# Early loading of two transposed h columns, and modulation blocks at groups 0, 1, 3, 4 of the backward middle stage

## The chip, the cores and the metric

The kernel runs on one core of a Trainium2 chip. The metric is the device time of one execution in microseconds (us). All results below are medians of fast runs, and each ratio is the mean time of one kernel's fast runs over the mean of the other kernel's fast runs of the same rounds, on the same chip; so it is not quite the ratio of the medians that stand beside it. The interval in brackets is a 95% interval. A run counts as slow when it is over 1.5% above the fastest of its kernel.

Terms: TensorE does the matrix products, into tiles of PSUM that ScalarE or VectorE then empties; SyncE issues nearly all DMAs (transfers between DRAM and the on-chip memory) here, one after the other. The granted clock is the share of TensorE's full clock in the profile. A filler is a product that is put between others only to keep TensorE busy.

## The reference

The reference runs a block with a Fourier filter and a squared-ReLU network forward, and returns its output and the gradients of nine inputs. Cut to what matters here:

```python
def _A_ref(x, w_r, w_i):                      # Fourier filter over (2048, 512)
    X = rfft2(x.astype(jnp.float32)) * (w_r + 1j * w_i)
    return irfft2(X, s=(S, D)).astype(jnp.bfloat16)

def _B_ref(x, w1, b1, w2, b2):                # D = 512, F = 1792
    h = jnp.einsum('bsd,df->bsf', x, w1) + b1
    r = jnp.where(h > 0, h, 0)
    return jnp.einsum('bsf,fd->bsd', r * r, w2) + b2

mod = (_silu(c) @ w_mod)                      # w_mod is (512, 6*512); six rows sa, ca, ga, sb, cb, gb
h = _layernorm(x) * (1 + ca) + sa;  x = x + ga * _A_ref(h, A_w_r, A_w_i)
h = _layernorm(x) * (1 + cb) + sb;  x = x + gb * _B_ref(h, ...)
# ... and jax.vjp of all this, for grad_out
```

Four parts of the backward pass matter. The **middle stage** runs the Fourier filter backwards in 8 groups of frequencies. Each group produces a gradient gW of the filter, which is stored. Products of the w1 gradient (grad_w1) are put between the groups to keep TensorE busy. The **modulation blocks** compute parts of the gradients of c and of w_mod, one block of 512 columns of w_mod each. **g1** is the inverse transform that follows the middle stage. The **last stage** takes pairs of row tiles, computes the gradient of x, and uses products of the w2 gradient (grad_w2) as TensorE's filler. Those products need transposed columns of h (hn), which a transposing DMA brings from DRAM.

## The kernel before

A modulation block, its two w_mod buffers (wmc) and its two output buffers (gwm):

```python
class GMod:                                   # self.bufs = 2
    def emit(self, jc, q, row, pool, ppool):
        nc.tensor.matmul(psb, lhsT=K["ones_sq"][q:q + 1, :], rhs=row, ...)
        nc.scalar.copy(out=gmbc, in_=psb)                                        # L459
        for dc in range(0, 4, 2):
            wmc = pool.tile([P, 2, D], BF16, name="wmc", bufs=self.bufs)
            nc.sync.dma_start(wmc, self.wm_view[:, dc:dc + 2, cs])               # L463
            gwm = pool.tile([P, 2, D], BF16, name="gwm", bufs=self.bufs)
            for i in range(2):
                if i == 0:
                    nc.scalar.activation(gwm[:, i, :], gmbc, AF.Copy, scale=...) # L467
                else:
                    nc.vector.tensor_scalar(gwm[:, i, :], gmbc, ...)             # L469
                nc.vector.scalar_tensor_tensor(out=junk, in0=wmc[:, i, :], ...,
                                               in1=gmbc, accum_out=...)          # L470 gm_junk
            nc.sync.dma_start(self.out9_view[:, dc:dc + 2, cs], gwm)             # L472
```

psb, the tile of the block's own product (L457), comes from the PSUM pool mmps with its two tiles named mm, which the products of grad_w1 and grad_w2 use, too.

The middle stage. All its loads and stores go through SyncE's one queue. In the profile gW is the gradient of the filter, gw at L1108 that of w1, and gw at L1176 that of w2:

```python
def grad_w1(fb, dc):
    for t in range(NT): nc.tensor.matmul(ps[:, 0:W4], ...)                       # L1104
    nc.scalar.copy(out=w1o[0][:, fb % 2, :], in_=ps[:, 0:W4])                    # L1108, gw1 has 2 buffers
    if fb % 2 == 1: nc.sync.dma_start(out4_view[...], w1o[0]...)                 # L1110
# ...
def ew_b(gi, G):
    cmul(nc, ew, Z[gi], G, ...)               # VectorE, L418 to L421
    gW = ew.tile([P, 2, 2, FP], BF16, name="gW", bufs=3)
    cmul(nc, ew, Xt[gi], G, gW[...], ...)
    for ...: nc.sync.dma_start(rows_, gW[...])                                   # L1146
def after_b(gi):
    if gi + 4 < 8: load(gi + 4)               # Z (L1133) and Xb (L1135)
    if gi == 4: nc.sync.dma_start(K["LG"], LG_dram)
    fill_w1(2 if 0 < gi < 6 else 1)
    if gi % 2 == 1: gms.pop(0)()              # a modulation block at groups 1, 3, 5, 7
```

The seam and the last stage:

```python
nc.sync.dma_start(g_sb, g_view)               # 2 MB, L1196
load_hn()                                     # transposing DMA, 512 KB, L1168
load_rows3(0); load_rows3(2)                  # rows n1 and gxl, L1193, L1194
for _ in range(3): load_hn()
spec_g1(tc, K, Z, CS)                         # L346; VectorE (L351) and ScalarE empty its PSUM tiles
# ... per pair of row tiles: q1 = gh1 * n1 (L1254), grad_w2 (L1173) as filler,
#     load_rows3(t + 4), and after the pair t == 10: grad_b2(), whose closing sum
#     (L1083) needs a ScalarE cast and a VectorE subtraction first
```

## Time and profile before

| | before |
|---|---|
| median of 3 runs | 433.97 us (431.92 to 434.96) |
| profiled span, mean granted TensorE clock | 432.7 us, 0.99 |
| TensorE, VectorE, ScalarE busy | 92%, 82%, 59% |
| last product of g1 ends | 350.36 us |
| last product of TensorE begins | 429.08 us |

A wait line reads: engine, instruction and line that waited, what released it, then total us, count and longest. In a timeline the columns are start, duration, engine, line, operation, output<-input, and in square brackets the idle time ahead with its releaser; SPq is SyncE issuing DMAs. In a table of stretches there follow, after the window, its length, the busy us of TensorE, its weight loads, VectorE, ScalarE and GpSimd (instruction counts in parentheses), the granted clock, the DMA share and GB/s. Two stretches of the kernel before that the prediction doesn't show, and that matter later:

```profile
315.00:325.00 10.00, 9.50 (x60) 5.33 (x58) 6.82 (x18) 2.58 (x6) 0.00 (x0) 1.00 0.96 313
345.00:355.00 10.00, 9.41 (x72) 6.47 (x72) 7.18 (x16) 6.17 (x12) 0.00 (x0) 1.00 0.82 275
```

TensorE is nearly full in both, at full clock.

### The profile page before, as it was taken

The page shows a single profiled execution, that of the slowest core. Times are in us where ns is not written, and L with a number is a line of the kernel's source. Part 1 is how long each engine was busy: PE and PEld are TensorE (multiplying, and loading weights), DVE is VectorE, ACT ScalarE, POOL GpSimd, SP SyncE. Part 2 cuts the span into 40 slices and gives each one's busy share as a digit, 9 for nine tenths or more (in the row PEclk, how much of TensorE's full clock was granted, in tenths as well). Part 3 has the DMA queues.
Part 4 walks back from the last instruction along what each step waited for, and adds up shares of the span by engine and source line. Part 5 has one row for each costly group of instructions (what it writes and reads, how often), then busy time and mean ns, then how long its engine had stood idle before and what let it go on. Part 6 is the DMA issues. An engine that isn't in the chain of part 4 may idle for free.

```text
span 432.7 us, 7098 instructions
## 1 busy us (share of the span) xinstructions
PE 398.7 (92%) x2353; PEld 196.1 (45%) x2375; DVE 353.7 (82%) x864; ACT 256.1 (59%) x487; POOL 40.9 (9%) x114
## 2 busy tenths in 40 slices
PE   2789999999899999999999999999999799995996
PEld 0344446654344444443444344455555464441332
DVE  6889768959995588969897998929577967989796
ACT  5578699679881286348536765465438374545231
POOL 7447930000000000000000000000000000000000
PEclk9999999999999999999999999999999999998899
DMA  9998899969595379779965997997995599999994
GB/s 237 222 293 278 223 282 273 318 222 188 177 360 191 121 127 329 186 162 226 276 189 158 210 330 271 245 244 217 263 300 160 166 245 257 255 257 255 247 246 137
DMA packets 147147, 101.11 MB, mean 234 GB/s; under 512 B 98945, under 2 KB 131590, under 8 KB 146726
## 3 DMA queue, kind: packets, MB, share of 16 engines
q1 hardware_dynamic: 145458, 98.01, 84.6%
q0 software_dynamic: 1088, 2.11, 2.1%
q10 hardware_dynamic: 564, 0.53, 0.4%
q8 instruction: 19, 0.31, 0.3%
q14 instruction: 18, 0.15, 0.1%
HBM read 35.44 MB, written 41.60 MB: 178 GB/s over the span
## 4 chain that ended last, share of the span: by engine, by line
PE 35%; DVE 25%; ACT 14%; DMA 12%; SPq 5%; issue 5%; POOL 2%; ACTq 0%; DVEq 0%
PE og L901 10%; PE mm L872 8%; PE mm L707 5%; PE mm L1173 4%; DMA out_dram<-gW 2%; PE psG L346 2%; ACT gab L712 2%; DVE gm_junk L470 2%; SPq L1168 2%; DMA n<-n_dram 2%; DMA out_dram<-gw 1%; DVE jk L1258 1%; ACT AE L329 1%; DMA y<-gx_dram 1%; DMA out_dram<-x 1%
## 5 line engine op out<-in xcount | busy, mean ns | idle before, releaser
L707 PE MATMUL mm<-gT,w2T 128*128 128x512 bf16 x224 | 57.8, 383 | 3.0 <-ACT gab L712 3.0
L1173 PE MATMUL mm<-g_sb,hn 128*128 128x512 bf16 x217 | 52.8, 394 | 3.3 <-DVE gw L1176 2.9
L872 PE MATMUL mm<-h2T,w 128*128 128x512 bf16 x224 | 53.4, 378 | 1.6 <-ACT r L874 1.4
L1104 PE MATMUL mm<-gab,h_sb 128*128 128x448 bf16 x256 | 51.4, 352 | 0.8 <-ACT gw L1108 0.8
L901 PE MATMUL og<-w1T,gab 128*128 128x512 bf16 x218 | 49.9, 379 | 1.0 <-DVE o L966 0.8
L901 PE MATMUL og<-w,h 128*128 128x512 bf16 x217 | 49.1, 379 | 0.3
L874 ACT ACTIVATE r<-mm,b1col 128x512 bf16<-128x512 f32 x56 | 37.0, 685 | 6.1 <-PE mm L872 3.3
L1173 PEld LDWEIGHTS <-hn 128*128 128x128 bf16 x224 | 21.6, 100 | 30.5 <-issue 8.2
L1104 PEld LDWEIGHTS <-h_sb 128*128 128x128 bf16 x256 | 24.6, 98 | 22.3 <-issue 1.7
L872 PEld LDWEIGHTS <-w 128*128 128x128 bf16 x224 | 21.1, 97 | 30.0 <-issue 8.3
L901 PEld LDWEIGHTS <-h 128*128 128x128 bf16 x224 | 21.8, 98 | 26.1 <-issue 0.9
L901 PEld LDWEIGHTS <-gab 128*128 128x128 bf16 x224 | 21.6, 98 | 25.9 <-issue 1.4
L707 PEld LDWEIGHTS <-w2T 128*128 128x128 bf16 x224 | 21.2, 98 | 22.4 <-issue 6.4
L914 ACT CAST G<-og 128x512 bf16<-128x512 f32 x16 | 9.2, 580 | 28.1 <-PE og L901 28.1
L876 DVE TENSOR_TENSOR h<-r 128x1024 bf16<-128x1024 bf16 x28 | 19.2, 687 | 4.8 <-ACT r L874 4.8
L1253 ACT ACTIVATE gs<-gn,inv 128x512 bf16<-128x512 bf16 x16 | 11.4, 716 | 18.6 <-DVE gn L1251 18.6
L712 ACT CAST gab<-mm 128x512 bf16<-128x512 f32 x36 | 21.4, 600 | 1.7 <-PE mm L707 1.5
L1108 ACT CAST gw<-mm 128x448 bf16<-128x448 f32 x16 | 8.7, 544 | 22.1 <-DMA out_dram<-gw 12.6
L418 DVE TENSOR_TENSOR p<-Z,G 128x1028 bf16<-128x1028 bf16 x8 | 5.6, 697 | 18.7 <-ACT G L313 10.1
L710 DVE CAST gab<-mm 128x512 bf16<-128x512 f32 x20 | 13.8, 688 | 7.3 <-PE mm L707 7.1
L377 ACT ACTIVATE Tsb<-psT 128x512 bf16<-128x512 f32 x32 | 18.5, 604 | 1.8 <-PE psT L375 1.5
L880 DVE TENSOR_TENSOR gab<-r,gab 128x1024 bf16<-128x1024 bf16 x28 | 19.2, 684 | 0.0
(289 smaller groups left out, 779.7 us busy)
## 6 DMA issues: line engine op xcount, KB each, us to landing
h_dram<-h SPq DMA_DIRECT2D x28, 256.0 KB, 3.6
gh_dram<-gab SPq DMA_DIRECT2D x28, 256.0 KB, 4.3
w<-in_B_w_dram SPq DMA_DIRECT2D x2, 1792.0 KB, 8.8
wmc<-in_w_mod_dram SPq DMA_DIRECT2D x12, 256.0 KB, 4.7
out_dram<-gwm SPq DMA_DIRECT2D x12, 256.0 KB, 3.3
wz_dram<-Z SPq DMA_DIRECT2D x8, 258.0 KB, 3.1
xs_dram<-Xs SPq DMA_DIRECT2D x8, 258.0 KB, 3.0
Z<-wz_dram SPq DMA_DIRECT2D x8, 258.0 KB, 4.1
```

The source lines that it names most:

```text
L377: nc.scalar.activation(Tsb, ps, AF.Copy, scale=EF_S)
L707: nc.tensor.matmul(ps, lhsT=w2T[:, dc, fc * P:(fc + 1) * P], rhs=gT[b][:, :, dc, :], start=(dc == 0), stop=(dc == 3))
L710: nc.vector.tensor_copy(out=gaT[b][:, fc, :], in_=ps)
L712: nc.scalar.copy(out=gaT[b][:, fc, :], in_=ps)
L872: nc.tensor.matmul(ps, lhsT=w1[:, dc, (fc + i) * P:(fc + i + 1) * P], rhs=h2T[b][:, :, dc, :], start=(dc == 0), stop=(dc == 3))
L874: nc.scalar.activation(r[:, i, :], ps, AF.Relu, bias=b1col[:, fc + i:fc + i + 1])
L876: nc.vector.tensor_tensor(h2, r, r, op=ALU.mult)
L880: K["gh"] = nc.vector.tensor_tensor(gh, r, gh, op=ALU.mult).ins
L901: nc.tensor.matmul(ps, lhsT=lhs(fc), rhs=rhs[:, fc, :], start=(fc == 0), stop=(fc == NFC - 1))
L1104: nc.tensor.matmul(ps[:, 0:W4], lhsT=h2_sb[:, t, dc * P:(dc + 1) * P], rhs=ghn[t // 4][:, t % 4, fs], start=(t == 0), stop=(t == NT - 1))
L1173: nc.tensor.matmul(ps, lhsT=hns[fc][:, t, :], rhs=g_sb[:, t, :], start=(t == 0), stop=(t == NT - 1))
L1253: nc.scalar.activation(gs[:, i, :], gn[:, i, :], AF.Copy, scale=inv1[:, t + i:t + i + 1], accum_out=rr[:, i, 0:1])
```

## The change

The intent: bring two of the 14 transposed columns while the DMA engines have room (behind the stores of group 5), so that the row loads of the last stage no longer stand behind a transpose at the seam; and move the modulation blocks out of groups 5 and 7, whose tail holds up VectorE and so g1.

```diff
+    hnp = tc.alloc_tile_pool(name="hnp", bufs=1, side="right")
+    hns, endp = [], {}
+    def load_hn():                                    # moved up; first two columns in hnp
+        ...
                 for p0_, n, rows_ in w_parts(o, gi):
-                    nc.sync.dma_start(rows_, gW[p0_:p0_ + n, i, :, 0:DF])
+                    K["gW"] = nc.sync.dma_start(rows_, gW[p0_:p0_ + n, i, :, 0:DF]).ins
 ...
             fill_w1(2 if 0 < gi < 6 else 1)
-            if gi % 2 == 1:
+            if gi == 5:
+                with tc.issue_after(K["gW"]):
+                    load_hn()
+                    load_hn()
+            if gi in (0, 1, 3, 4):
                 gms.pop(0)()
 ...
     nc.sync.dma_start(g_sb, g_view)
-    load_hn()
     load_rows3(0)
     load_rows3(2)
-    for _ in range(3):
+    for _ in range(2):
         load_hn()
```

The pools are cut here.

More of the change, by code (lines that the diff above doesn't have):

```diff
@@ L1049 @@
     gm = GMod(tc, K, scf, gsc, wm_view, out9_view)
+    hnp = tc.alloc_tile_pool(name="hnp", bufs=1, side="right")
+    hns, endp = [], {}
+    def load_hn():
+        fc = len(hns)
+        if fc < NFC:
+            pool = hnp if fc < 2 else endp.get("hn", endp["gw"])
+            hns.append(pool.tile([P, NT, P], BF16, name="hn", bufs=2 if pool is not endp.get("hn") else 4))
+            nc.sync.dma_start(hns[fc], h_dram[fc, :, :], transpose=True)
     lf2 = tc.alloc_tile_pool(name="lf2", bufs=1, side="right")
@@ L1160 @@
     g_sb = gwp.tile([P, NT, D], BF16, name="g_sb")
-    hns, endp = [], {}
-    def load_hn():
-        fc = len(hns)
-        if fc < NFC:
-            hns.append(endp.get("hn", gwp).tile([P, NT, P], BF16, name="hn", bufs=4))
-            nc.sync.dma_start(hns[fc], h_dram[fc, :, :], transpose=True)
+    endp["gw"] = gwp
     def grad_w2(fc):
@@ L1307 @@
     gwp.release()
+    hnp.release()
     h2p.release()
```

## The prediction

> **What bounds the kernel now.** I read the engine totals first: TensorE is busy for 92% of the span, VectorE for 82%. So TensorE's gaps are what a change can win, and the next question is where they lie. I cut the second half into stretches. The columns are busy microseconds of TensorE, its weight loads, VectorE, ScalarE and GpSimd, then the granted clock, the DMA share and GB/s:
>
> ```profile
> 285.00:295.00 10.00, 10.00 (x112) 5.72 (x111) 3.87 (x9) 5.46 (x11) 0.00 (x0) 1.00 0.83 258
> 305.00:315.00 10.00, 10.00 (x70) 5.94 (x68) 5.12 (x12) 5.74 (x11) 0.00 (x0) 1.00 0.96 288
> 325.00:335.00 10.00, 9.66 (x63) 5.64 (x63) 7.47 (x19) 8.83 (x17) 0.00 (x0) 1.00 0.50 144
> 335.00:345.00 10.00, 8.04 (x80) 4.88 (x79) 10.00 (x25) 4.01 (x7) 0.00 (x0) 1.00 0.57 166
> 390.00:398.00 8.00, 3.55 (x24) 1.42 (x23) 7.08 (x17) 4.74 (x11) 0.00 (x0) 0.94 1.13 257
> 398.00:405.00 7.00, 7.00 (x19) 2.18 (x18) 4.65 (x14) 1.83 (x4) 0.00 (x0) 0.58 1.00 268
> ```
>
> The middle stage on the way back runs from about 283 us to 338 us. TensorE is full there, because the products of the w1 gradient fill the gaps between the groups: nothing done inside the stage can shorten it. Its tail (335 to 345) has VectorE full and TensorE not; the DMA engines are half idle from 325 to 345, then full. Around 395 there is a hole in TensorE's work, followed by a lowered clock.
>
> Second, the waits, with the total, the count and the longest:
>
> ```profile
> PE psG L346 <- DVE utcs L351: 1.9, 1, 1.9
> ACT gw L1108 <- DMA out_dram<-gw: 12.6, 2, 7.1
> DVE q L1254 <- DMA gxl<-gx_dram: 2.3, 1, 2.3
> DVE q L1254 <- DMA n<-n_dram: 2.1, 2, 1.1
> PE mm L1173 <- DVE gw L1176: 2.9, 1, 2.9
> ```
>
> The first says that TensorE stands at the inverse transform (g1) because VectorE has not emptied its PSUM tile. The third and fourth say that VectorE, which paces the last stage, waits for rows. The last is the hole at 395.
>
> Third, the chain that ended last, at the seam of the two stages:
>
> ```profile
> 342.25 0.67 DVE gm_junk L470 x2
> ...
> 344.12 0.67 DVE gm_junk L470 x2
> 344.79 0.62 DVE utcs L351
> 345.44 0.60 PE psG L346 x4
> ...
> 348.28 7.24 SPq L1168
> 355.57 1.28 SPq L1193
> 356.90 3.30 DMA gxl<-gx_dram
> 360.20 0.68 DVE q L1254
> ```
>
> This is the heart of it. The fourth modulation block (gm_junk) stands on VectorE ahead of the first emptying of g1, which frees TensorE. Then SyncE needs 7.24 us to issue the first transposed h column (L1168), and the row loads of the last stage (L1193, L1194) are queued behind it; VectorE gets its rows at 360.20.
>
> **What the Trainium skill says.** "Perfetto Trace Analysis", section 'What "DMA-bound" means', counts an issuing engine whose sequencer is solid with DMA slices as a bound of its own. The trace agrees for the last stage: from 358.3 to 417.9 us the 13 remaining column transposes hold SyncE for 8.60+3.76+2.49+5.51+3.93+4.13+4.10+2.48+3.54+2.12 = 40.7 us of 59.6. "DMA: Bandwidth & Descriptors", section "Rules for kernel authors", advises to issue a DMA early and wait for it late, which is this change; section "Issuing engines are not separate DMA queues" says that all DMAs share the same 16 engines, so an early load is free only where these have room (0.50 and 0.57 above, but 0.96 from 305 to 315). "TensorE: Matmul & The Clock Gate", section "What's actually happening", gives the half clock after an idle window of about 3.4 us. The trace fits: gaps of 1.5 and 2.9 us between 391.7 and 398, then a clock of 0.58, and 16 matmuls in 1.86+4.54 = 6.4 us that take 3.6 elsewhere.
>
> **The change part by part.**
> (a) Two of 14 transposes move from the seam to behind the stores of group 5. Each brings 512 KB (128 x 2048 bf16); the record of L1168 has 2.0 to 7.2 us of SyncE, median 3.3, and a median 6.1 us to landing. Group 5's stores end at 333.6 us. Two transposes at 2.5 to 3.3 us (the DMA engines are half free) hold SyncE until about 339.5. Behind them wait the stores of groups 6 and 7 (about 2.5 us of issue each, before: 338.2 to 344.4). SyncE also loses the last modulation block's issues there (about 3 us between 333.7 and 337.4, 1.1 at 344.5). So the stores of group 7 end near 344.5, as before, and the 2 MB load of g_sb, which waited for such a store to land (1.8 us), is issued at 347 to 348, as before (347.87).
> (b) After g_sb the row loads follow at once, so at about 348.5 instead of 355.57: 7 us earlier in issue. They queue in the DMA rings behind g_sb: 2 MB at the 377 GB/s of the stretch 350 to 355 is 5.6 us, so the first rows land at about 355.5. VectorE's q starts there instead of at 360.20, some 4.5 us earlier, if g1 is done in time, which is (c).
> (c) The modulation blocks move from groups 1, 3, 5, 7 to 0, 1, 3, 4. One costs VectorE four products of 0.746, four read-outs of 0.082 and two scalings of 0.348: 4.0 us by the sum, 3.34 us elapsed, since they overlap (331.27 to 334.61). ScalarE pays 0.59+2x0.72 = 2.0 us, TensorE 0.39, and 1 MB is moved. Groups 5 to 7 lose two blocks: VectorE's group 6 can start when its G is there (about 331.5 to 333 instead of 334.61), group 7 ends at about 339.5 instead of 342.2, and the first emptying of g1 starts there instead of at 344.70: 4 to 5 us earlier. TensorE then loses the stalls of 1.95 and 0.45 us in g1, and the transform (now done at 352) is done by about 348, so that the unfolding is no longer what holds q. In groups 0 to 4 the blocks fall where VectorE waits for ScalarE (4.9 us at 306 to 311, 5.25 us at 322 to 327), so they should be hidden.
> (d) The last stage has 12 transposes instead of 14, about 2x3.3 us of SyncE and 1 MB less, while its DMA share is 1.0 to 1.1. So its row loads come earlier, too, and the VectorE waits of 2.1 us on n should shrink.
>
> **The sum.** Only TensorE's gaps can be won. From 337 us to its last product they are 0.45+1.95 (g1), 0.15, 0.44, 1.5, 2.9, plus 6.4-3.6 = 2.8 us lost to the clock: 10.2 us. The floor is 434-10 = 424. The first two, 2.4 us, I count fully. Of the 7.2 us around 391 to 405 (two gaps and the clock) I count half, 3.6: VectorE comes some 4.5 us earlier into the last stage, TensorE some 2.4, so VectorE gains a lead of only 2 us, and it is full from 366 to 397. I take off 0.5 for friction in groups 0 to 4. That is 5.5 us: **428.5 us**.
>
> **Rivals.**
> 1. *SyncE and ScalarE choke in groups 0 to 4.* A block needs two buffers of w_mod columns that the block before must free, and each landing takes 4.7 us. Blocks in adjacent groups (0 and 1, 3 and 4) put such waits into the one queue that also stores gW and the w1 gradient, and ScalarE already waited 7.1 us for one of these stores. The DMA engines stand at 0.96 from 305 to 325. For it: TensorE lost 0.83 us behind that wait. Against it: TensorE always had filler. It would cost 1 to 4 us: 430 to 433.
> 2. *The new transposes hold up SyncE.* If each takes 4 us or more, the stores of group 7 and with them g_sb come 3 to 4 us later, and the rows land where they did. The gain is then the g1 part and a little more: 431.
> 3. *The last stage is bound by TensorE's work or by the DMA engines anyway.* From 405 us on TensorE is full. If the hole at 395 only moves, the earlier start is worth 2.4 to 3 us: 431.
> 4. *The hole closes entirely*, with its clock loss, as VectorE's lead suffices: 424 to 425.
>
> **Range and chances.** Most weight lies between rivals 2 and 3 (431) and rival 4 (424.5), about 428.5 in the middle; rival 1 sets the upper end. Range 424 to 433. Faster by over 2% means below 425.5, nearly the whole of the floor: 0.15. Slower by over 2% would need new stalls of 9 us: 0.03. Within 2%: 0.82.
>
> **What would show it.** Right: no wait of psG on utcs; VectorE's first q at 355 to 357; L1193 issued within 2 us of g_sb; the two early transposes at 333 to 340; about 5 us shorter gaps of TensorE after 337, and its clock nearer to 1 at 395 to 405. Wrong: SyncE's stores of group 7 ending after 346, TensorE below 9.5 in a stretch from 285 to 335, or the wait on gw (2.9 us) still there with the clock loss.

## More of the kernel before

The medians of the kernel before differed between rounds from 432.4 to 434.6 us, which is why ratios and not differences of medians decide.

The diff moves lines: grad_w1 is L1114 after, its ScalarE copy L1118, its store L1120, the gW stores L1156, the transposes L1058, the rows L1201 and L1202, g_sb L1204, grad_w2 L1181, its scaling by VectorE L1184, the closing sum of b2 L1093, q L1261. The block keeps its lines (L457 to L472), and so does g1 (L346, L351).

## The result and the profile after

The change made the kernel slower: 440.13 us (439.95 to 441.8, 4 runs) against 434.46 us (431.92 to 434.96, 4 runs), ratio 1.0151 [1.0103, 1.0199]. The predicted 428.5 us, and its range up to 433, were missed on the slow side. The same work is done (TensorE 399.6 us busy, before 398.7); the time is in new gaps. From the start of the middle stage (283 us) to the end of g1, TensorE's gaps of 0.4 us or more add up to 9.0 us, before 3.2 us. g1 ends at 357.03 us instead of 350.36, 6.7 us later, and the last product begins at 434.40 instead of 429.08, 5.3 us later: the last stage gives 1.4 us back. The order of instructions on each engine is not the same in the two kernels: with the blocks other things moved. After the end of g1 48 products of the w1 gradient are left instead of 37, and in the last stage some products of grad_w2 and of the b2 sum stand at other places.

The stretches of the kernel after:

```profile
315.00:325.00 10.00, 5.75 (x23) 2.63 (x23) 4.03 (x12) 4.93 (x9) 0.00 (x0) 0.83 0.94 247
335.00:345.00 10.00, 10.00 (x77) 6.37 (x75) 7.79 (x20) 5.42 (x11) 0.00 (x0) 1.00 0.49 150
345.00:355.00 10.00, 5.33 (x48) 3.56 (x46) 8.12 (x17) 2.12 (x5) 0.00 (x0) 0.83 0.86 177
```

TensorE stands for over 4 us in two of them, and each time the clock falls as well. The prediction's own sign of failure, "TensorE below 9.5 in a stretch from 285 to 335", is there in the first. The waits of the kernel after in the second half name both gaps and what led to them:

```profile
DVE gm_junk L470 <- DMA wmc<-in_w_mod_dram: 9.0, 3, 3.6
ACT gw L1118 <- DMA out_dram<-gw: 8.6, 2, 6.6
ACT gwm L467 <- DMA out_dram<-gwm: 4.9, 3, 3.3
PE psG L346 <- DVE utcs L351: 4.7, 1, 4.7
PE mm L1114 <- ACT gw L1118: 4.3, 1, 4.3
DVE gwm L469 <- DMA out_dram<-gwm: 3.6, 2, 2.6
```

The first, third and sixth line hardly exist in the kernel before (none of them reaches 0.5 us there). All three are waits of a modulation block for its buffers: VectorE for w_mod columns to land, ScalarE and VectorE for the gwm store of the block before. The fourth was 1.9 us and the fifth 0.8 us before. The second is not new: before, ScalarE waited 12.6 us for these stores.

**The first gap, read backwards.** Two lines of ScalarE's timeline and four of SyncE's, kernel after:

```profile
302.76 0.72 ACT L467 ACTIVATE gwm<-gmbc,scf 128x512 bf16<-128x512 bf16 x1 [3.26 <-DMA out_dram<-gwm]
...
318.67 0.53 ACT L1118 CAST gw<-mm 128x448 bf16<-128x448 f32 x1 [6.58 <-DMA out_dram<-gw]
```

```profile
294.51 4.32 SPq L1156 DMA_DIRECT2D out_dram<-gW  x6
...
299.40 0.91 SPq L472 DMA_DIRECT2D out_dram<-gwm  x2
...
310.04 2.54 SPq L1156 DMA_DIRECT2D out_dram<-gW  x4
...
315.07 0.38 SPq L1120 DMA_DIRECT2D out_dram<-gw  x1
```

The block of group 1 wants the gwm buffers of the block of group 0. Their store was issued only at 299.40, behind six gW stores that hold SyncE from 294.51 for 4.32 us. So ScalarE waits 3.26 us for it and starts L467 at 302.76. ScalarE works in order: the conversion of group 2's transform stands behind this wait and comes at 305.40 (before 300.51). Group 2's gW is then ready later, and SyncE, which also works in order, stands waiting for it until 310.04 (before 308.51). The w1 gradient store that is behind these stores and two more loads goes out only at 315.07, ScalarE waits 6.58 us for its buffer until 318.67, and TensorE, which needs ScalarE to empty its PSUM tile, stands 4.33 us from 314.92. The next 32 matmuls then take 7.64 us, where 32 of them had taken 6.21 us from 306.94, so the lowered clock costs 1.4 us more.

**Why the filler failed there.** Before, ScalarE had waited even longer for such a store, 7.07 us up to 324.75, and TensorE lost only 0.83 us. Two lines of TensorE's timeline before, then two after:

```profile
321.32 3.19 PE L1104 MATMUL mm<-gab,h_sb 128*128 128x448 bf16 x16
325.33 3.19 PE L1104 MATMUL mm<-gab,h_sb 128*128 128x448 bf16 x16 [0.83 <-ACT gw L1108]
```

```profile
313.09 0.39 PE L457 MATMUL mm<-grow,ones_sq 1*128 1x512 bf16 x1
...
319.25 7.64 PE L1114 MATMUL mm<-gab,h_sb 128*128 128x448 bf16 x32 [4.33 <-ACT gw L1118]
```

Before, the wait fell in group 4, which has no block: of the two mm tiles one was free, and TensorE had 3.19 us of filler. After, it falls in group 3, which has a block: one tile waits to be emptied behind the store, the other holds the block's product, whose emptying (L459, at 319.10) stands behind the same wait of ScalarE. So no filler fits. In e2, e3 and e4 below, the gaps behind ScalarE's copy stand at the same place, after L457 and the group's transforms. No run gives the block a PSUM tile of its own: this is read from the order and the code, and not tested.

**The second gap.** The blocks of groups 3 and 4 wait for their w_mod columns until 320.21, 325.74 and 337.21. SyncE issued the load for the last only at 333.21, behind four gW stores of 330.64, for which it had stood idle since 324.8; by the order of its products, VectorE had done with that buffer at about 321.9. VectorE ends group 7 at 349.5 instead of 342.2, so the first emptying of g1 comes late and TensorE stands 4.67 us (345.5 to 350.15), the fourth line of the waits above. Here, too, the clock falls: the next 12 matmuls of g1 take 2.72 us, where 16 take 1.92. The block at group 7 that was to be cleared away was worth 1.9 us there; its replacement costs more.

The early transposes themselves came late, too: they are ordered behind the stores of group 5, which went out at 341.64, so they hold SyncE for 4.54 us from 344.21, g_sb is issued at 357.35 (before 347.87), and the first q stands 1.80 us for rows and begins at 367.09 (before 360.19). The stores of group 7 end at 354.66, the second of the prediction's signs of failure (after 346); the third, the wait of 2.9 us on gw, is gone, but in its place the closing sum of b2 waits 2.8 us.

### The profile page after: what moved, and what is told of

It reads as the page before. It is cut to its first block, busy times and chain, and to the rows that moved or that the text cites. A ratio compares the mean times of both kernels' runs of the same rounds, so it can differ in the third digit from the quotient of the medians.

```text
span 438.1 us, 7088 instructions
## 1 busy us (share of the span) xinstructions
PE 399.6 (91%) x2353; PEld 196.9 (45%) x2375; DVE 355.5 (81%) x864; ACT 256.5 (59%) x487; POOL 41.1 (9%) x114
## 4 chain that ended last, share of the span: by engine, by line
PE 44%; DVE 22%; ACT 16%; DMA 10%; issue 4%; POOL 2%; SPq 1%; ACTq 0%; DVEq 0%
PE og L901 11%; PE mm L872 10%; PE mm L1181 6%; PE mm L707 4%; PE mm L1114 3%; DVE gm_junk L470 2%; DMA xs_dram<-Xs 2%; PE psG L346 2%; DMA wmc<-in_w_mod_dram 2%; ACT gab L712 2%; DVE p L419 2%; ACT AE L329 1%; DVE p L418 1%; ACT Xs L313 1%; DMA out_dram<-gx 1%
## 5 line engine op out<-in xcount | busy, mean ns | idle before, releaser
L1114 PE MATMUL mm<-gab,h_sb 128*128 128x448 bf16 x256 | 52.1, 359 | 4.3 <-ACT gw L1118 4.3
L1181 PE MATMUL mm<-g_sb,hn 128*128 128x512 bf16 x217 | 50.8, 385 | 0.5 <-DMA gxl<-gx_dram 0.2
L1114 PEld LDWEIGHTS <-h_sb 128*128 128x128 bf16 x256 | 25.0, 99 | 27.3 <-issue 6.9
L1181 PEld LDWEIGHTS <-hn 128*128 128x128 bf16 x224 | 21.5, 99 | 26.1 <-issue 2.6
L470 DVE SCALAR_TENSOR_TENSOR gm_junk<-wmc,onef,gmbc 128x512 bf16<-128x512 bf16 x24 | 17.9, 748 | 15.0 <-DMA wmc<-in_w_mod_dram 9.0
L1260 ACT ACTIVATE gs<-gn,inv 128x512 bf16<-128x512 bf16 x16 | 11.4, 715 | 22.9 <-DVE gn L1258 22.9
L1118 ACT CAST gw<-mm 128x448 bf16<-128x448 f32 x16 | 8.7, 541 | 19.9 <-PE mm L1114 10.0
```

The lines of the kernel that those rows point to most:

```text
L470: nc.vector.scalar_tensor_tensor(out=junk, in0=wmc[:, i, :], scalar=K["onef"], in1=gmbc, op0=ALU.mult, op1=ALU.mult, accum_out=self.gsc[:, ...
L1114: nc.tensor.matmul(ps[:, 0:W4], lhsT=h2_sb[:, t, dc * P:(dc + 1) * P], rhs=ghn[t // 4][:, t % 4, fs], start=(t == 0), stop=(t == NT - 1))
L1181: nc.tensor.matmul(ps, lhsT=hns[fc][:, t, :], rhs=g_sb[:, t, :], start=(t == 0), stop=(t == NT - 1))
```

## The experiments

All runs are correct against the reference unless said. "Alt" below means that the second and the fourth block take their gwm buffers from another pool with two buffers of its own, so that no block waits for the gwm store of the block just before it. There is one thing that I could not build: three or four buffers for wmc or gwm in their own pool, since the on-chip memory has no room there (no run shows this). In their traces e1, e5, both e7, e10 and e11 have the order of the kernel before on TensorE, VectorE and ScalarE, and e2 has that of the kernel after; e4, e6, e9 and e12 have one of their own on some engines.

| run | what | us | ratio to before | gaps of TensorE (0.4 us or more) from 283 us to the end of g1, us |
|---|---|---|---|---|
| before | | 432.4 to 434.6 | 1 | 3.2 |
| after | both parts | 440.13 | 1.0151 | 9.0 |
| e1_loads_only | early loads, blocks at 1, 3, 5, 7 | 435.93 | 1.0070 | 6.0 |
| e2_blocks_only | blocks at 0, 1, 3, 4 alone | 438.53 | 1.0149 | 8.5 |
| e3_gwm_alt | after + alt | 440.44 | 1.0173 | 7.7 |
| e4_0246 | after, blocks at 0, 2, 4, 6 | 436.25 | 1.0072 | 5.2 |
| e5_loads_gwm_alt | e1 + alt | 433.47 | 0.9980 | 3.3 |
| e6_no_waits | after + alt, no wait for w_mod | 432.57 | 0.9973 | 3.4 |
| e7_loads_g4 | e1, loads behind group 4 | 432.04 | 0.9951 | profile slow |
| e7_loads_g4_alt | the same + alt | 431.91 | 0.9941 | 0.9 |
| e9_b2_later | the same, closing sum of b2 later | 432.00 | 0.9942 | 3.3 |
| e10_rows_first | e7 alt, rows before g_sb | 432.80 | 0.9947 | 2.7 |
| e11_rows_pool | e7 alt, rows issued by GpSimd | 430.79 | 0.9938 | 1.9 |
| e12_later_pool | e9 and e11 together | 430.33 | 0.9933 | profile slow |

### Each half alone: e1 and e2

```diff
 e1_loads_only (against after)           e2_blocks_only (against before)
-            if gi in (0, 1, 3, 4):      -            if gi % 2 == 1:
+            if gi % 2 == 1:             +            if gi in (0, 1, 3, 4):
```

> The changed kernel with its modulation blocks put back at groups 1, 3, 5, 7; only the two early transposes are left of the change. Theory A (the blocks in adjacent groups cause the loss, the early loads are worth a little): 430 to 434 us, no TensorE gap of 4.3 us near 319 us, row loads of the last stage issued right behind g_sb. Rival B (the early transposes hold up SyncE and cause the loss): 438 to 442 us, with the stores of group 7 ending after 350 us.

> The kernel before with only the modulation blocks moved to groups 0, 1, 3, 4; the column loads stay at the seam. Theory A: 439 to 444 us, with a TensorE gap of about 4.3 us near 315 to 320 us and another in g1 of about 4.7 us. Rival B: 432 to 435 us, as before.

The blocks alone make as large a loss as both parts: 438.53 us, ratio 1.0149 [1.0076, 1.0222], with both gaps (3.4 us behind ScalarE's copy of the w1 gradient, 5.1 us in g1) and 9.2 us of waits for w_mod columns. But the early loads alone are no gain either: 435.93 us, 1.0070 [1.0024, 1.0115], between the ranges of both theories. The reason stands in SyncE's timeline of e1, and in its waits:

```profile
333.78 5.78 SPq L1058 DMA_TRANSPOSE hn<-h_dram  x2
339.68 1.03 SPq L472 DMA_DIRECT2D out_dram<-gwm  x2
```

```profile
PE psG L346 <- ACT utcs L353: 4.6, 1, 4.6
```

The two transposes hold SyncE where and for as long as the prediction said, but the gwm stores of the block of group 5, at 333.66 us before, now go out at 339.68, behind them. The last block waits for those buffers on ScalarE (4.1 us), the emptying of g1 that ScalarE has to do stands behind this wait, and TensorE stands 4.6 us.

### More gwm buffers: e3 and e5

```diff
-            gwm = pool.tile([P, 2, D], BF16, name="gwm", bufs=self.bufs)
+            gwm = (pool2 or pool).tile([P, 2, D], BF16, name="gwm", bufs=self.bufs)
```

> The changed kernel with the same order of instructions on every engine, but the second and fourth modulation block write their gwm tiles into two other buffers, so they no longer wait for the stores of the block before. Theory A1 (the loss starts with these buffer waits: ScalarE 4.9 us, VectorE 3.6 us): both waits vanish, G of group 2 is ready about 4 us earlier, the TensorE gap of 4.3 us near 319 shrinks under 1 us, 434 to 437 us. Rival A2 (the order of the one queue and the landing of the w_mod loads, VectorE's 9.0 us of waits on wmc, carry the loss): the wmc waits stay at 8 to 10 us, 438 to 441 us.

> The early loads alone (blocks at 1, 3, 5, 7), same order of instructions on every engine as in the run with the loads only, but two more gwm buffers, so that the fourth block doesn't wait for the gwm stores that stand behind the two transposes. Theory A (the early loads cost time only because those stores, issued 6 us later, hold ScalarE for 4.1 us and so g1 on TensorE for 4.6 us): both waits go, the time falls by 4 to 6 us against the loads-only run, to 429 to 432, below the kernel before. Rival B (the transposes cost SyncE's time itself, through g_sb and the row loads): 433 to 436 us, TensorE's gap in g1 replaced by another.

In e5, with the order of e1 on every engine, the wait for gwm is gone and with it the loss: 433.47 us, 0.9980 [0.9939, 1.0021]. But Theory A isn't borne out whole. The time lies in the range of rival B, and TensorE's gap in g1 is replaced by another one of 3.3 us, behind VectorE (4.6 us in e1): the last block's w_mod load is issued behind the two transposes as well, at 338.03 (before 334.29), and VectorE waits 1.7 us for it. So the wait for gwm made part of e1's loss; how much, two rounds on different chips don't tell. In e3, where TensorE, VectorE, ScalarE and SyncE have the same instructions in the same order as in the kernel after (but for one neighbouring pair on ScalarE), the gwm waits are gone as well, and yet it gains nothing: 440.44 us, 1.0173 [1.0126, 1.0220]; the gaps are 2.9 us (after: 4.3) and 4.7 us. The waits of e3 show where it went:

```profile
DVE gm_junk L470 <- DMA wmc<-in_w_mod_dram: 13.1, 5, 3.6
```

VectorE's wait for w_mod columns grew from 9.0 to 13.1 us. The wait that was taken away was spent at another one, with the loads of the columns in the same SyncE order. So the theory that the gwm buffers alone explain the kernel after fell here.

### Blocks two groups apart: e4

```diff
-            if gi in (0, 1, 3, 4):
+            if gi % 2 == 0:
```

> The changed kernel with the blocks at groups 0, 2, 4, 6: as far apart as before, each one group earlier. Theory A (adjacent blocks share two buffers and that is the cost): 430 to 435 us, waits on wmc and gwm under 2 us together. Rival C (what costs is any block in the early groups, where the DMA engines are full, adjacent or not): 437 us or more, with the TensorE gap still there.

436.25 us, 1.0072 [1.0034, 1.0110]: about half of the loss is back. The wait of g1 on VectorE is 0.5 us instead of 4.7. The waits for w_mod columns (9.9 us in 3) are not gone: they lie at groups 2 and 4, VectorE is busy for only 0.73 us from 305 to 315, and TensorE stands 2.3 and 2.5 us behind ScalarE's copies. Neither theory's range holds (up to 435, from 437). That the blocks are adjacent thus makes some of the loss, but the run doesn't divide it cleanly: it also puts a block back to group 6. Both gaps behind ScalarE's copies lie right after a block's product, at groups 2 and 4, where ScalarE waits 5.9 and 6.1 us for the w1 store; in the kernel before, its waits of 5.6 and 7.1 us fall in the same groups, and there is no block in them. That fits the two PSUM tiles above; it was not tested.

### Without the waits: e6

```diff
 (after + alt)
-   in0=wmc[:, i, :], scalar=K["onef"], in1=gmbc
+   in0=(gmbc if self.bufs == 2 else wmc[:, i, :]), scalar=K["onef"], in1=gmbc
```

> Wrong on purpose in the gradient of c: the changed kernel with two more gwm buffers, and the products of the first four blocks read gmbc twice instead of the loaded w_mod columns; the loads are still made, but nothing waits for them. Theory A (adjacent blocks cost through the waits of VectorE for the w_mod loads and of ScalarE for the gwm buffers): VectorE's waits of 9 to 13 us on wmc are gone, TensorE's gaps of 4.3 us near 319 and 4.7 us in g1 are gone or under 1 us each, 428 to 433 us. Rival C (the DMA traffic and the queue positions of the blocks in groups 0 to 4 cost, whoever waits): 436 us or more.

This kernel is wrong: one output (the gradient of c) has a relative error of 8e4, because the blocks multiply by gmbc instead of w_mod. All the loads are still made; the wait for them is gone, together with the wait for gwm. But more than the waits changed: with no one reading the columns, SyncE's and VectorE's instructions come in another order (TensorE's is that of the kernel after), and the second block's loads go out at 286.81 instead of 305.53. It takes 432.57 us, 0.9973 [0.9907, 1.0039], which is 7.6 us under the kernel after (by medians of different rounds). Its waits up to the end of g1:

```profile
PE mm L1114 <- ACT gw L1118: 2.6, 2, 1.6
PE psG L346 <- DVE utcs L351: 0.8, 1, 0.8
```

So the blocks' work fits into groups 0 to 4, as the prediction had it; what doesn't fit is their waits for buffers and what these do to the order. The two can't be told apart here. And even without these the kernel is within its interval of the kernel before, not 5.5 us faster. That leaves a second question: where did the gain in the last stage go?

### Loads behind group 4: e7

```diff
 (against e1; e7_loads_g4_alt also has alt)
-            if gi == 5:
+            if gi == 4:
                 with tc.issue_after(K["gW"]):
```

> Blocks at 1, 3, 5, 7 as before; the two column loads behind the stores of group 4 instead of group 5, where SyncE idled for 2.7 us in the kernel before. Theory A: the gwm stores of the third block come at about 336 instead of 339.7, ScalarE's wait shrinks from 4.1 to under 1.5 us and TensorE's in g1 with it: 430 to 433 us, level with the kernel before or up to 1% better. Rival: the stores of w1 gradients and of group 5 behind the transposes hold ScalarE earlier, TensorE loses 2 us or more between 325 and 337: 434 to 437 us.

> As the run with the loads behind group 4, with two more gwm buffers. Theory A: no wait on a gwm store is left, 428 to 432 us, the best so far or level with the loads behind group 5 with those buffers. Rival: same as without the buffers, because the gwm stores no longer matter there.

432.04 us, 0.9951 [0.9901, 1.0001], one slow run of 514 us left out (its profile is of that run, and isn't used); and 431.91 us, 0.9941 [0.9893, 0.9989] with alt, one slow run of 438.6 us left out. The two are alike, as the rival of the second had it. One group earlier there is no block right behind the transposes, whose gwm stores they could hold up. In the profile of e7_loads_g4_alt only 0.9 us of gaps are left up to the end of g1; but e9, e10 and e11, which have the same middle stage, show 3.3, 2.7 and 1.9 us, no less on the whole than the kernel before (3.2), so the 0.9 us are this execution's luck. SyncE and VectorE of the kernel with alt at the seam:

```profile
348.07 0.35 SPq L1204 DMA_DIRECT2D g_sb<-in_grad_out_dram  x1
348.47 0.42 SPq L1201 DMA_DIRECT2D n<-n_dram  x1
...
350.53 11.38 SPq L1058 DMA_TRANSPOSE hn<-h_dram  x2
```

```profile
357.57 0.69 DVE L1261 TENSOR_TENSOR q<-gh,n 128x1024 bf16<-128x1024 bf16 x1 [0.61 <-DMA gxl<-gx_dram]
```

Now the rows are issued at 348.47, 7.1 us earlier than before, as the prediction's step (b) said. But q comes only 2.6 us earlier, and the next two transposes hold SyncE for 11.38 us, where before four of them took 7.24+8.60 = 15.84 us. In the last stage a hole stays, of 4.4 us where the kernel before has 1.5 and 2.9 us:

```profile
PE mm L1093 <- DVE gn L1269: 2.6, 1, 2.6
PE mm L1181 <- DVE gw L1184: 1.8, 1, 1.8
```

### Where the hole comes from: e9, e10, e11, e12

All four start from e7_loads_g4_alt.

```diff
 e9_b2_later: the closing sum of b2 one unit of grad_w2 later
-        later.append(add)
+        later.append(lambda: later.append(add))
-        while later:
+        for _ in range(len(later)):
             later.pop(0)()
 e10_rows_first
+    load_rows3(0)
+    load_rows3(2)
     nc.sync.dma_start(g_sb, g_view)
-    load_rows3(0)
-    load_rows3(2)
 e11_rows_pool (both row loads)
-            nc.sync.dma_start(rows3[t][0], n1_dram[:, t:t + 2, :])
+            nc.gpsimd.dma_start(rows3[t][0], n1_dram[:, t:t + 2, :])
```

> The kernel with the two transposes behind group 4 and two more gwm buffers (431.94 us, ratio 0.994 to the kernel before), with one thing changed: the closing sum of grad_b2 (two matmuls that need a ScalarE cast and a VectorE subtraction first) comes one unit of the w2 gradient later. Every kernel so far has a hole in TensorE's work at about 389 to 398 us (2.6 us ahead of these two matmuls, then 1.8 us behind VectorE's gw, clock 0.72 after it), early loads or not. Theory A (the hole comes from the place of this sum in TensorE's order): the 2.6 us gap goes, at least half of the hole of 4.4 us closes, the clock in 395 to 405 rises to 0.9 or more, time 428 to 430.5. Theory B (the step of the prediction: the hole comes from VectorE that is late because its rows are late): a gap of 3 us or more stays near 390 to 400 in front of other matmuls, time within 0.5 us of 431.9.

> The same kernel (two transposes behind group 4, two more gwm buffers), but the first four row loads of the last stage are issued before the 2 MB load of g_sb and not after it. Prediction's step b said that rows issued 7 us earlier land about 5 us earlier; measured, they landed only 2.6 us earlier (q at 357.6 after a wait of 0.6 us). Theory A (they queue behind the 2 MB of g_sb in the rings): rows land at 353 to 355, no wait of q for gxl, and q starts when its input from the transform is there, at 355 to 357; g_sb lands about 3 us later; time 431 to 432.5, since the hole near 391 stays whatever the start. Theory B (the start of VectorE's work decides the end): the time falls by as much as q comes earlier, 1 to 2 us, and the hole near 391 shrinks.

> The same kernel (two transposes behind group 4, two more gwm buffers), but all row loads of the last stage are issued by GpSimd, which is idle, instead of SyncE, where they stand behind the column transposes; instructions of TensorE, VectorE and ScalarE are the same in the same order. Theory A (what the last stage loses to SyncE's transposes is only what its row loads wait behind them, and little of that sets the end): the waits of q for n and gxl (2.5 and 0.6 us) go, the hole near 391 stays at 3 us or more, time 430.5 to 432. Theory B (the step d of the prediction: SyncE's queue in the last stage paces VectorE and with it the end): the waits go and the hole with them, time 427 to 430. A miss would be rows that land later than before because GpSimd's issue is slower.

> Both changes of the last stage together on the kernel with two transposes behind group 4 and two more gwm buffers: the closing sum of grad_b2 one unit of the w2 gradient later (alone: no gap of 2.6 us, clock 1.00 from 385 to 415, ratio 0.994), and all row loads of the last stage on GpSimd's queue (alone: no waits of VectorE for rows, ratio 0.994). Theory A (two separate causes of the hole at 390 to 400: the place of the sum in TensorE's order, and VectorE behind with gw): of TensorE's gaps of 4.4 us only one of 1 to 2 us behind gw is left, the clock stays at 0.95 or more from 395 to 405, time 427 to 430, ratio about 0.988. Theory B (whatever closes here opens elsewhere in the last stage, which is paced by VectorE, busy 9 us of 10 from 365 to 415): gaps of 3 us or more remain in the last stage and the ratio stays at 0.992 to 0.996.

**e9**: the gap of 2.6 us ahead of the closing sum is gone, and the clock held at 1.00 up to 415 us. The same stretch in e7_loads_g4_alt, then in e9:

```profile
395.00:405.00 10.00, 8.87 (x32) 3.15 (x33) 8.28 (x20) 5.28 (x12) 0.00 (x0) 0.72 0.98 259
```

```profile
395.00:405.00 10.00, 7.41 (x38) 2.72 (x36) 9.99 (x25) 6.49 (x15) 0.00 (x0) 1.00 1.13 256
```

The busy time is lower in the second because the clock is higher: more instructions are done in it. From the end of g1 to the last product it is 74.2 us, in e7_loads_g4_alt 77.1, both with 37 products of w1 left. One large gap remains: 1.8 us behind gw, with VectorE full (9.99). So the first half of the hole goes with the place of that sum in TensorE's order: by the code its first matmul needs a ScalarE cast and its second a VectorE subtraction, and everything behind it waits along (the kernel after has both waits by name, 0.6 and 2.8 us). But this shows in one profile alone: the median is 432.00 us, ratio 0.9942 [0.9899, 0.9984], the same as without it. In the trace Theory A was borne out, in time Theory B.

**e10**: the rows don't wait for g_sb, and the first q has no wait for rows any more, but it comes no earlier:

```profile
358.48 0.69 DVE L1261 TENSOR_TENSOR q<-gh,n 128x1024 bf16<-128x1024 bf16 x1
```

In this execution g1 ended at 351.03 (in e7_loads_g4_alt 349.42), and the chain runs through ScalarE's copy and the unfolding: q now waits for its other input. Counted from the end of g1, q begins after 7.5 us, in e7_loads_g4_alt after 8.2 and in the kernel before after 9.8. 432.80 us, 0.9947 [0.9895, 0.9999]. So the wait went as Theory A said, but q's start and the time (431 to 432.5) did not quite come out. In its six runs the time goes with the clock: 429.0 and 430.2 us in the two at a mean clock of 1.00, 433.8 to 434.1 in the three at 0.990 to 0.992 (in e12, though, one run at 1.00 took 433.6).

**e11**: with the rows on GpSimd's queue, TensorE, VectorE and ScalarE have the same instructions in the same order. The waits of q for rows shrink to 0.24 us. A hole of 3.3 us stays (e7_loads_g4_alt: 4.4):

```profile
390.75 0.38 PE L1093 MATMUL mm<-b,ones_col 128*1 128x512 bf16 x1 [1.36 <-DVE gn L1269]
...
394.48 1.68 PE L1181 MATMUL mm<-g_sb,hn 128*128 128x512 bf16 x4 [1.93 <-DVE gw L1184]
```

430.79 us, 0.9938 [0.9888, 0.9987]: Theory A, that little of what the rows wait for behind SyncE's transposes sets the end.

**e12**: 430.33 us and ratio 0.9933 [0.9878, 0.9988] by the four of its six runs that count as fast (427.4 to 433.6); its profile fell on a slow run (435.4 us). The two slow runs (434.2 and 435.4 us) have the clock of many fast ones, 0.991; with them the ratio of the means is 0.997. So there is no step to the 0.988 that Theory A wanted; Theory B's ratio came out. From e7 to e12 no kernel is distinguishable from another; all are some 0.6% faster than the kernel before (for e7_loads_g4 the interval reaches 1.0001), and none by 2%.

## Why the prediction was wrong

**The step that failed is (c), its sentence on groups 0 to 4: "In groups 0 to 4 the blocks fall where VectorE waits for ScalarE [...], so they should be hidden", with 0.5 us in the sum.** It counted VectorE's work and asked whether there was idle time for it. e6 shows that this was right of the work. But the idle time that it found (4.9 and 5.25 us) was itself the end of a wait: ScalarE stood 5.6 and 7.1 us for a w1 store then, and a block needs ScalarE, too. And the block's buffers weren't counted: each block needs both of its wmc and both of its gwm buffers back, their loads and stores stand in SyncE's one order behind gW stores that wait for VectorE, and ScalarE and VectorE wait in order for them with the next group's work behind. The waits measured 17.5 us on VectorE and ScalarE (9.0+4.9+3.6), and on TensorE two gaps of 4.3 and 4.7 us and a clock loss of 1.4 us after the first. That the blocks' places make the loss is shown by e2; that it is by their waits for buffers is read from the trace, and e6, which takes the waits away and also changes the order, brought back 7.6 us.

The prediction had this as **rival 1**, with the right mechanism, and with "TensorE always had filler" against it. The filler itself fell: grad_w1 needs ScalarE to empty PSUM and a store to give gw1 back, both stood in the queues that were choked, and the block's own product took the second PSUM tile. The term was mis-sized: 1 to 4 us, where e2 measured 1.5% of 433 us, some 6.5 us.

By the prediction's other steps:

- **(a) Two transposes behind group 5 are harmless.** The place and length were right where the middle stage ran in time (e1: 333.78, 5.78 us; the prediction: 333.6 to 339.5); the stores of groups 6 and 7, put at 2.5 us each, took 6.3 us together in the kernel before and 5.2 in e1. What was missed is who stands behind them: not only the stores of groups 6 and 7 but also the gwm stores of the block at group 5, which the block at group 7 waits for (e1: 4.1 us on ScalarE, 4.6 us on TensorE). In the kernel after there is no such block, but the stage itself was late, and the transposes with it (344.21). Rival 2's sign came in e1, too: g_sb was issued at 351.69 instead of 347.87, with transposes of 2.9 us each where the rival asked for 4.
- **(b) Rows issued 7 us earlier, q 4.5 us earlier.** The issue was right once the middle was repaired (e7_loads_g4_alt: 348.47, the prediction 348.5). q came 2.6 us earlier, not 4.5. The two limits stand next to each other: the rows behind g_sb, and the unfolding of g1, as e10 shows, where the rows were there and q was no earlier.
- **(c) Group 7 ends 4 to 5 us earlier and g1's stalls of 2.4 us go.** VectorE ended group 7 at 349.5 and the stalls grew to 4.7 us. With the blocks left where they were and the loads behind group 4 they are 0.9 and 0.3 us in e7_loads_g4_alt, but 1.9 to 2.1 us in e9, e10 and e11, as in the kernel before: no run shows that they go.
- **(d) SyncE has 2 x 3.3 us less in the last stage.** The two transposes behind g_sb take 11.4 us where four had taken 15.84: about 4.5 us less, and what is gained there doesn't show: VectorE's waits on n, 2.1 us before, are 1.5 to 2.8 us in e1, e5, e7_loads_g4_alt, e9 and e10. e11 frees the rows from SyncE entirely and gains nothing that the times show.
- **The sum: 3.6 us from the hole at 391 to 405, through VectorE's earlier start.** Part of this came. A hole stays in each kernel with the early loads, and e9 shows that its first gap belongs to the order of the b2 sum. But from the end of g1 to the last product it takes 78.7 us in the kernel before, and in the kernels with the early loads and the same order on TensorE, VectorE and ScalarE 75.9 (e1), 75.2 (e5), 77.1 (e7_loads_g4_alt), 77.4 (e10) and 75.3 (e11): 1.3 to 3.5 us less, one execution each. This is of the size of the 0.6% (2.6 us) of e7 to e12. Which waits it comes from isn't shown. The kernels with the blocks moved can't be compared with these, as their order in the last stage is another one. Between themselves they show no gain: 75.8 us in e2, which has no early load, and 77.4 in the kernel after, where the transposes came late.
- **The half clock.** The prediction says that the trace fits an idle window of about 3.4 us. Neither gap is that long (1.52 and 2.93 us, with 1.8 us of matmuls between them), so its trace shows that the clock fell and not that this is why.

What remains open: how the loss divides between wmc and gwm waits (taking one away moved it to the other, e3), what would be gained with three or four buffers or a PSUM tile of the block's own, which no run tries, and why the b2 change shows in the trace of e9 and not in its median. The spread of the runs within a kernel (up to 5 us in e10, 6 us in the fast runs of e12) is as large as what is looked for.

## What to carry to other kernels

Idle time of the engine that does the work is not enough to move a block there: write down each buffer that it takes, in PSUM, too, what gives it back, and what stands ahead of that in its queue. And ask why the engine is idle there: it may be waiting for another that the block needs as well. Two blocks that share two buffers need at least the round of store, landing and reload between them, and in an in-order queue this round includes whatever waits ahead. And before a gain is counted in a later stage, ask what that stage's hole waits for: here about half of it was a sum placed in TensorE's order ahead of its inputs, which no earlier load could mend.

## What the Trainium skill lacked or had wrong

- "DMA: Bandwidth & Descriptors", section "Issuing engines are not separate DMA queues", says that the time on the sequencer to initiate a DMA "is usually small relative to the DMA itself". For transposes these runs differ: two of 512 KB held SyncE for 5.22 us behind group 4 (e7_loads_g4_alt), 5.78 us behind group 5 (e1), and 11.38 us behind the 2 MB load of g_sb. The page gives no sequencer time for a transpose of this size from DRAM, nor does it say that the same two can take twice as long at another place; that the 2 MB ahead of them are the reason was not tested.
- The same page, section "Rules for kernel authors", advises to issue early and wait late. It lacks the other side, that an early DMA stands in the order of its engine's queue ahead of stores which others wait for: in e1, behind 5.78 us of transposes, a store went out at 339.68 us instead of 333.66, and TensorE stood 4.6 us.
- "Perfetto Trace Analysis", section "DMA Optimizations", says that balancing DMAs over the engines may help if descriptor generation is the bottleneck. Here GpSimd took all row loads at 0.54 to 0.60 us each, and VectorE's waits for rows fell to 0.24 us, but the time was the same (0.9938 and 0.9941). SyncE was issuing for 62.6 of 68 us from 350 us on even so, and no issue of it is in the chain that ended last from 345 us on: a solid sequencer need not be on the path.
- "TensorE: Matmul & The Clock Gate", section "What's actually happening", gives an idle window of about 3.4 us, free-running. The gaps of 4.33 and 4.67 us, with a clock of 0.83 in their stretches, fit it. But in the kernel after a gap of 2.79 us at 401.4 us, after one of 0.59 us, was enough for 16 matmuls to take 4.57 us instead of 3.63, and in e9 a gap of 1.81 us was not. It may be that a few matmuls between two gaps don't count as busy; how busy a window must be, the page doesn't say, and I didn't test it.
- No page says that waits of this kind can move on: with the gwm waits gone (e3) the wmc waits rose from 9.0 to 13.1 us, and the time stayed.
